# Another PSUM place for two outputs, and an order of steps written anew, in a gated linear attention with an ELU layer

## The chip, the cores and the metric

The kernel runs on one core of one Trainium2 chip. The metric is the device time of one execution in microseconds (us). TensorE (PE, its weight loads PEld), VectorE (DVE), ScalarE (ACT), GpSimd (POOL) and SyncE (SP, which here only issues DMAs) run side by side and meet through semaphores.

## What is computed

The attention has 4 sequences, 8 heads, 768 positions and 48 values a head. In each head a complex state S of 48 x 48 decays by a complex gate a, takes in the outer product of k and v, and is read by q:

```
scale = minimum(mag, 0.999) / (mag + 1e-6)      # mag = |a|
new_re = ar * S_re - ai * S_im                  # ar, ai: gate times scale
new_im = ar * S_im + ai * S_re
S_re, S_im = new_re + kv, new_im                # kv = k[t] outer v[t]
y[t] = q[t] @ S_re
```

Heads side by side give 3072 rows of 384 values, x. Then h = x @ w_in (384 x 2048), g = h where h > 0 and exp(h) - 1 elsewhere, and the result is g @ w_out (2048 x 384). All of it is float32.

## The kernel before

The work is cut into 12 units. A unit is 128 positions of two sequences (NB = 2, numbered n). For each unit the kernel goes from gates to attention, from attention to x, and from x through the two layers.

**Gates.** `squares` (L709, L710) squares the parts of the gate, `joined` (L716) adds them, `logarithms` (L735, L736) and `powers` (L746, L747) form logarithms and exponentials on ScalarE; `lengths` (L772), `ratios` (L759, L760) and `slopes` (L780) are VectorE operations for the first four units, and `ratios` and `joined` are POOL's later. `angles` (L815) is an arctangent on ScalarE and `carried` (L821) adds what came over from the unit before in the sequence. `turns` (`turned`, L832) sums the angles down the positions by a matmul for each n and takes off whole turns on VectorE (L837, L840); its last row goes to a later unit by a POOL DMA (L856). `quartered` (L883) sums the logarithms by matmuls, `quarters_used` (L898) exponentiates them; both are called by `decays` for unit 2 and by `valued` of the unit before for later ones. `waves` (L967 to L971) makes sines and cosines, `scaled` (L981, L982) and `gated` (L993) multiply k and q. `ends` (L951) brings decays at chunk ends into a tile T by way of DRAM.

**Attention.** `transposed` (L1013, copied by ScalarE at L1014) turns q and k over; `state_products` (L1054) and `state_sums` (L1069 on VectorE, L1071 on POOL) carry the states; `scored` (L1126, masked at L1134) makes scores, `valued` the values (L1087) and what the states add (L1096), and ScalarE copies the outcome to x and y (L1157, L1158). `seam` (L1170) moves 16-row pieces of y into their places in x by DMA: three from POOL, three from another queue.

**Layers.** `inner(u, f)` (L1190) is six matmuls of w_in with x, `elu` (L1199 to L1201) makes g. For units 0 and 1 `project(u, n, f0, f1)` (L1211) accumulates g @ w_out for output n over slices f0 to f1 of 16 and, at the last, copies it through two `o` buffers (L1219) to DRAM (L1220). From unit 2 on, folded matmuls (`folded`, `combined`, `product`, L1254 to L1320) take the place of `project`.

**PSUM.** `work` gives tiles from two rings of three: "w" for small results and transposes, and "mlp" for the layers. The tag "y" is one tile of two banks (`[C, 2, 512]`), which scores and values take in turn. A tile that comes round again waits for the last reader of the tile that lay there. Of the four outputs that `project` accumulates, (0, 0), (1, 0) and (0, 1) lie in "mlp", and (1, 1) in "w". SBUF tiles of the gates ("n") come from a ring of six.

**Order.** Each engine works strictly through its instructions in the order in which the program issues them. `first` is a list, written by hand, of calls up to the end of unit 3's gates; `convert` in it takes one step in rounding the weights. After `first`, `plan` sorts steps by due times, and every later unit has the same slots.

Of the kernel before, what the change touches and what calls it, by code (L numbers as in the profile page):

```python
# [10 lines left out]
FP32 = mybir.dt.float32  # L11
# [5 lines left out]
C = 128  # L17
# [488 lines left out]
def kernel(  # L506
# [14 lines left out]
    DM, DF = moe_w_in.shape[0], moe_w_out.shape[0]  # L521
# [3 lines left out]
    NB = 2  # L525
# [11 lines left out]
    ps = ctx.enter_context(tc.tile_pool(name="ps", bufs=1, space=PSUM))  # L537
# [33 lines left out]
    def work(shape, tag="w"):  # L571
        return ps.tile(shape, FP32, tag=tag, bufs=3, name=tag)
# [4 lines left out]
    def where(u):  # L577
        return u % (B // NB) * NB, u // (B // NB) * C
# [114 lines left out]
    def new(tag, bufs=1, shape=None):  # L693
        return sb.tile(shape or [C, NB, H, D], FP32, tag=tag, bufs=bufs, name=tag)
# [510 lines left out]
    def project(u, n, f0, f1):  # L1205
        x = nat[u]
        assert ("out", (f1 - 1) // WF) in done
        if f0 == 0:
            x["o", n] = work([C, DM], "w" if (u, n) == (1, 1) else "mlp")
        for f in range(f0, f1):  # L1210
            nc.tensor.matmul(  # L1211
                x["o", n], lhsT=x["g", f // 8][:, f % 8, ts(n, C)], rhs=w_out[:, f],
                start=(f == 0), stop=(f == NF - 1),
            )
        if f1 == NF:
            b, s = where(u)
            for m in range(2):
                o = new("o", 2, [C, HN])
                nc.scalar.copy(out=o, in_=x["o", n][:, ts(m, HN)])  # L1219
                nc.sync.dma_start(out=out[ds((b + n) * S + s, C), ts(m, HN)], in_=o)  # L1220
# [197 lines left out]
    def gates_of(u, *at):  # L1418
# [37 lines left out]
        (begun, 2), (squares, 2), *2 * [(convert,)], (inner, 1, 8), (inner, 1, 10), (joined, 2),  # L1456
        (convert,), (inner, 1, 12), (fetch, "out", 6), (fetch, "out", 7), *2 * [(convert,)],
        (elu, 1, 8), (convert,), (project, 0, 0, 0, 4), (convert,), (elu, 1, 10),
        *3 * [(convert,)], (elu, 1, 12), (load_qk, 2), *4 * [(convert,)], (inner, 1, 14),
        (elu, 1, 14), (logarithms, 2), (powers, 2), *4 * [(convert,)], (project, 1, 0, 0, 4),  # L1460
        (project, 1, 1, 0, 4), *3 * [(convert,)], (noted, 2), (lengths, 2), (ratios, 2),
        (slopes, 2), (load_a, 3), (angles, 2), (carried, 2), (convert,), (project, 0, 1, 0, 4),
        (convert,), (project, 0, 0, 4, 8), *3 * [(convert,)], (decays, 2), (project, 0, 1, 4, 8),
        *2 * [(convert,)], (turns, 2), (project, 0, 0, 8, 12), (begun, 3), *4 * [(convert,)],
        (project, 1, 0, 4, 8), (waves, 2), (scaled, 2), *2 * [(convert,)], (gated, 2), (ends, 2),
        (load_qk, 3), (squares, 3), *2 * [(convert,)], (project, 1, 1, 4, 8), *4 * [(convert,)],
        (joined, 3), (states, 2, 0), *5 * [(convert,)], (project, 0, 0, 12, 16),
        (transposed, 2, "q", 0), (transposed, 2, "k", 0), (project, 0, 1, 8, 12),
        (transposed, 2, "q", 1), (transposed, 2, "k", 1), (logarithms, 3),
        (project, 1, 1, 8, 12), (scored, 2), (project, 0, 1, 12, 16), (powers, 3), (lengths, 3),  # L1470
        (ratios, 3), (slopes, 3), (angles, 3), (project, 1, 1, 12, 16), (carried, 3),
        (valued, 2), (turns, 3), (project, 1, 0, 8, 12), (seam, 2), (noted, 3), (waves, 3),
        (project, 1, 0, 12, 16), (scaled, 3), (ends, 3), (opened,),
    ]
    def layer_of(u, at_h, at_p):
        for m in range(NF // 2):
# [72 lines left out]
```

## Time and profile before

| what | us |
|---|---|
| median of three runs | 688.48 (686.95 to 689.6) |
| profiled execution | 688.77 |
| its span, first to last instruction | 687.0 |
| PE busy | 661.4 |
| PEld busy | 579.5 |
| DVE busy | 400.5 |
| ACT busy | 396.0 |
| POOL busy | 183.4 |

Busy time is what an engine worked, so several can add up to more than the span. In a timeline a row is a run of like instructions: start, duration, engine, line, output and inputs, how many; in brackets the engine's idle time ahead of it and what ended it. A float32 matmul is two records, so four matmuls of `project` are eight records. Times count from the start of the span. The granted clock is the share of full speed at which TensorE was let run.

### The profile page before, as it was taken

The page shows a single profiled execution, that of the slowest core. Times are in us where ns is not written, and L with a number is a line of the kernel's source. Part 1 is how long each engine was busy: PE and PEld are TensorE (multiplying, and loading weights), DVE is VectorE, ACT ScalarE, POOL GpSimd, SP SyncE. Part 2 cuts the span into 40 slices and gives each one's busy share as a digit, 9 for nine tenths or more (in the row PEclk, how much of TensorE's full clock was granted, in tenths as well). Part 3 has the DMA queues.
Part 4 walks back from the last instruction along what each step waited for, and adds up shares of the span by engine and source line. Part 5 has one row for each costly group of instructions (what it writes and reads, how often), then busy time and mean ns, then how long its engine had stood idle before and what let it go on. Part 6 is the DMA issues. An engine that isn't in the chain of part 4 may idle for free.

```text
span 687.0 us, 15760 instructions
## 1 busy us (share of the span) xinstructions
PE 661.4 (96%) x6656; PEld 579.5 (84%) x6656; DVE 400.5 (58%) x584; ACT 396.0 (58%) x620; POOL 183.4 (27%) x199
## 2 busy tenths in 40 slices
PE   8899899898999999999999999999999999999996
PEld 6777785465889889889889889989989989989996
DVE  5898999815785564564564564654654653642151
ACT  6875455645747657557557557557557557541230
POOL 2000000100233433424424424524524523501000
PEclk9899999899999999999999999999999999999998
DMA  9985655430731741731741731651641631200000
GB/s 167 179 147 91 148 174 160 78 58 25 125 57 53 122 66 54 117 69 53 115 74 52 112 76 51 111 80 51 108 81 50 127 65 49 52 2 7 24 1 29
DMA packets 149899, 55.98 MB, mean 81 GB/s; under 512 B 129172, under 2 KB 142652, under 8 KB 149820
## 3 DMA queue, kind: packets, MB, share of 16 engines
q1 hardware_dynamic: 146336, 53.57, 40.2%
q0 software_dynamic: 3264, 1.18, 1.5%
q8 instruction: 54, 0.88, 0.6%
q14 instruction: 25, 0.20, 0.1%
q10 hardware_dynamic: 220, 0.14, 0.1%
HBM read 48.88 MB, written 4.78 MB: 78 GB/s over the span
## 4 chain that ended last, share of the span: by engine, by line
PE 77%; ACT 1%; issue 1%; DVE 0%; DVEq 0%; ACTq 0%
PE mlp L1190 30%; PE mlp L1296 27%; PE w L1013 5%; PE y L1126 3%; PE w L1054 3%; PE y L1096 3%; PE mlp L1211 3%; PE w L832 2%; PE y L1087 1%; PE w L883 1%; PE w L1211 0%; PE mlp L1054 0%; ACT o L1219 0%; ACT L898 0%; ACT L746 0%
## 5 line engine op out<-in xcount | busy, mean ns | idle before, releaser
L1190 PE MATMUL mlp<-x,w_in 128*128 128x256 f32 x1152 | 262.3, 382 | 2.9 <-DVE g L1201 2.6
L1190 PEld LDWEIGHTS mlp<-x,w_in 128*128 128x128 f32 x1152 | 215.7, 191 | 32.5 <-DVE g L1201 3.0
L1199 ACT ACTIVATE ee<-mlp 128x512 f32<-128x512 f32 x96 | 57.3, 596 | 139.3 <-PE mlp L1190 133.4
L1201 DVE SCALAR_TENSOR_TENSOR g<-ee,mlp 128x512 f32<-128x512 f32 x96 | 65.6, 685 | 119.8 <-ACT ee L1200 107.7
L1296 PE MATMUL mlp<-w_out,g 128*128 128x192 f32 x640 | 110.3, 326 | 0.0
L1296 PEld LDWEIGHTS mlp<-w_out,g 128*128 128x128 f32 x640 | 105.5, 190 | 2.7
L1274 DVE TENSOR_TENSOR g<-g 128x512 f32<-128x512 f32 x80 | 67.4, 842 | 2.7
L1200 ACT ACTIVATE ee<-ee 128x512 f32<-128x512 f32 x96 | 60.5, 630 | 2.8
L1071 POOL TENSOR_TENSOR S<-S,T 128x384 f32<-128x384 f32 x36 | 29.2, 829 | 104.0 <-DVE S L1069 104.0
L1296 PE MATMUL mlp<-w,g 128*128 128x192 f32 x320 | 55.8, 329 | 0.0
L1296 PEld LDWEIGHTS mlp<-w,g 128*128 128x128 f32 x320 | 52.1, 190 | 0.6
L1170 POOL DMA_DIRECT2D x<-y x62 | 30.4, 498 | 70.4 <-ACT y L1111 37.1
L1315 ACT COPY o<-mlp 128x192 f32<-128x192 f32 x10 | 3.2, 318 | 66.0 <-DMA out_dram<-o 32.6
L856 POOL DMA_DIRECT2D carry<-n x10 | 5.0, 504 | 130.5 <-DVE n L840 130.5
L898 ACT ACTIVATE n<-w 64x384 f32<-64x384 f32 (+1 forms) x60 | 28.1, 486 | 18.4 <-PE w L883 17.7
L993 POOL TENSOR_TENSOR kg<-k,cs 128x1536 f32<-128x1536 f32 x8 | 34.9, 4360 | 10.8 <-issue 10.7
L1211 PE MATMUL mlp<-w_out,g 128*128 128x384 f32 x96 | 34.4, 509 | 1.5 <-DVE g L1201 1.5
L716 POOL TENSOR_TENSOR n<-n 128x768 f32<-128x768 f32 x8 | 16.5, 2060 | 69.7 <-ACT n L710 69.7
L1211 PEld LDWEIGHTS mlp<-w_out,g 128*128 128x128 f32 x96 | 18.7, 199 | 15.0 <-issue 2.7
L759 POOL TENSOR_TENSOR n<-ar,n 128x768 f32<-128x768 f32 x8 | 14.9, 1858 | 61.0 <-ACT n L747 61.0
L1296 PE MATMUL mlp<-wt,g 128*128 128x192 f32 x160 | 29.4, 327 | 0.0
L1014 ACT COPY qt<-w 128x512 f32<-128x512 f32 x48 | 25.5, 581 | 5.7 <-PE w L1013 5.7
(173 smaller groups left out, 989.7 us busy)
## 6 DMA issues: line engine op xcount, KB each, us to landing
w<-in_moe_w_out_dram SPq DMA_DIRECT2D x8, 768.0 KB
g<-in_moe_w_in_dram SPq DMA_DIRECT2D x16, 384.0 KB
g<-in_moe_w_out_dram SPq DMA_DIRECT2D x16, 384.0 KB
w<-in_moe_w_in_dram SPq DMA_DIRECT2D x16, 288.0 KB
vn<-in_v_dram SPq DMA_DIRECT2D x24, 192.0 KB
out_dram<-o SPq DMA_DIRECT2D x48, 96.0 KB
ar<-in_a_re_dram SPq DMA_DIRECT2D x22, 192.0 KB
ai<-in_a_im_dram SPq DMA_DIRECT2D x22, 192.0 KB
```

What stands on the lines that cost most here:

```text
L898: nc.scalar.activation(out=flat(x[key][to, n : n + 1]), in_=t[of], func=AF.Exp, scale=sign)
L993: eng.tensor_tensor(out=to[:, :, :, 0:D], in0=each.unsqueeze(2).to_broadcast([C, step * H, 2, D]), in1=x["cs"][:, n * H : (n + step) * H], ...
L1013: nc.tensor.transpose(t[:, h], of, ident)
L1071: eng.tensor_tensor(out=new_s, in0=new_s, in1=wide, op=ALU.mult)
L1170: eng.dma_start(out=x["x"][ds(j * HP + D, G), i], in_=x["y"][ds(j * HP + i * G, G)])
L1190: nc.tensor.matmul(t[:, e], lhsT=w_in[:, i, ts(f + e, C)], rhs=x["x"][:, i], start=(i == 0), stop=(i == NI - 1),)
L1199: nc.scalar.activation(out=e, in_=t, func=AF.Relu, scale=-1.0)
L1200: nc.scalar.activation(out=e, in_=e, func=AF.Exp, scale=-1.0)
L1201: nc.vector.scalar_tensor_tensor(out=x["g", f // 8][:, f % 8 : f % 8 + 2], in0=e, scalar=-1.0, in1=t, op0=ALU.add, op1=ALU.max)
L1211: nc.tensor.matmul(x["o", n], lhsT=x["g", f // 8][:, f % 8, ts(n, C)], rhs=w_out[:, f], start=(f == 0), stop=(f == NF - 1),)
L1274: nc.vector.tensor_tensor(out=S_of(u, k, h), in0=a, in1=b, op=op)
L1296: nc.tensor.matmul(to, lhsT=a[:, m], rhs=b[:, m], start=(first and h == 0 and m == 0), stop=False, skip_group_check=True,)
```

## The change

Outputs of unit 1 no longer come from the two rings. The first call of `project` for unit 1 allocates a "y" tile and gives output 0 its first bank and output 1 its second; outputs of unit 0 stay in "mlp".

```diff
         if f0 == 0:
-            x["o", n] = work([C, DM], "w" if (u, n) == (1, 1) else "mlp")
+            if u == 0:
+                x["o", n] = work([C, DM], "mlp")
+            elif n == 0:
+                t = ps.tile([C, NB, 512], FP32, tag="y", bufs=1, name="y")
+                for m in range(NB):
+                    x["o", m] = t[:, m, 0:DM]
```

The end of `first` is written anew. Unit 1's projections are all done ahead of the scores of unit 2, and unit 0's later slices come after; unit 3's squares stand ahead of unit 2's waves, its logarithms and exponentials right after, its turns ahead of unit 2's values. No step is added or left out. (Units count from 0: the second unit is 1, the fourth is 3.)

```diff
-        (convert,), (project, 0, 0, 4, 8), *3 * [(convert,)], (decays, 2), (project, 0, 1, 4, 8),
-        *2 * [(convert,)], (turns, 2), (project, 0, 0, 8, 12), (begun, 3), *4 * [(convert,)],
-        (project, 1, 0, 4, 8), (waves, 2), (scaled, 2), *2 * [(convert,)], (gated, 2), (ends, 2),
-        (load_qk, 3), (squares, 3), *2 * [(convert,)], (project, 1, 1, 4, 8), *4 * [(convert,)],
-        (joined, 3), (states, 2, 0), *5 * [(convert,)], (project, 0, 0, 12, 16),
-        (transposed, 2, "q", 0), (transposed, 2, "k", 0), (project, 0, 1, 8, 12),
-        (transposed, 2, "q", 1), (transposed, 2, "k", 1), (logarithms, 3),
-        (project, 1, 1, 8, 12), (scored, 2), (project, 0, 1, 12, 16), (powers, 3), (lengths, 3),
-        (ratios, 3), (slopes, 3), (angles, 3), (project, 1, 1, 12, 16), (carried, 3),
-        (valued, 2), (turns, 3), (project, 1, 0, 8, 12), (seam, 2), (noted, 3), (waves, 3),
-        (project, 1, 0, 12, 16), (scaled, 3), (ends, 3), (opened,),
+        (convert,), (project, 0, 0, 4, 8), *3 * [(convert,)], (decays, 2), (project, 1, 0, 4, 8),
+        *2 * [(convert,)], (project, 1, 1, 4, 8), (turns, 2), *2 * [(convert,)],
+        (project, 0, 1, 4, 8), (begun, 3), (squares, 3), *2 * [(convert,)],
+        (project, 1, 0, 8, 12), (waves, 2), (scaled, 2), (joined, 3), (gated, 2), (ends, 2),
+        (load_qk, 3), (logarithms, 3), (powers, 3), (convert,), (project, 1, 1, 8, 12),
+        *4 * [(convert,)], (states, 2, 0), *5 * [(convert,)], (project, 1, 0, 12, 16),
+        (transposed, 2, "q", 0), (project, 1, 1, 12, 16), (transposed, 2, "k", 0), (lengths, 3),
+        (ratios, 3), (slopes, 3), (transposed, 2, "q", 1), (angles, 3), (project, 0, 0, 8, 12),
+        (transposed, 2, "k", 1), (carried, 3), (project, 0, 1, 8, 12), (scored, 2), (turns, 3),
+        (project, 0, 0, 12, 16), (valued, 2), (seam, 2), (noted, 3), (waves, 3),
+        (project, 0, 1, 12, 16), (scaled, 3), (ends, 3), (opened,),
```

The calls of `convert` after the last weights are rounded do nothing. In the order of instructions that the changed program builds, every instruction of the old one is there, and the engines' orders differ only between the sums of logarithms of unit 2 (L883) and the first `inner` of unit 2 (L1190).

## Prediction

> **What bounds the kernel now.** I read the page first, then the chain of waits, then TensorE's timeline between 105 and 176 us, and the timelines of the other engines there.
>
> ```profile
> span 687.0 us, 15760 instructions
> ...
> PE 661.4 (96%) x6656; PEld 579.5 (84%) x6656; DVE 400.5 (58%) x584; ACT 396.0 (58%) x620; POOL 183.4 (27%) x199
> ...
> PE 77%; ACT 1%; issue 1%; DVE 0%; DVEq 0%; ACTq 0%
> ```
>
> TensorE bounds it, so the change can only win where TensorE idles or runs slowly. From 175.87 on the chain is matmuls alone; before that stands the stretch that the change rewrites:
>
> ```profile
> 122.28 2.85 PE L1211 MATMUL mlp<-w_out,g 128*128 128x384 f32 x8
> 127.36 1.65 PE L832 MATMUL w<-n,sum_turns 128*128 128x384 f32 x2 [2.23 <-ACT n L898]
> 129.37 1.65 PE L832 MATMUL w<-n,sum_turns 128*128 128x384 f32 x2 [0.36 <-ACT n L898]
> 130.81 6.91 PE L1211 MATMUL mlp<-w_out,g 128*128 128x384 f32 x16
> ...
> 164.43 1.99 PE L1096 MATMUL y<-qt,S 128*48 128x64 f32 x64
> 168.42 0.88 PE L832 MATMUL w<-n,sum_turns 128*128 128x384 f32 x2 [2.00 <-DVE n L821]
> 169.96 0.91 PE L832 MATMUL w<-n,sum_turns 128*128 128x384 f32 x2 [0.66 <-ACT n L898]
> 170.71 5.32 PE L1211 MATMUL mlp<-w_out,g 128*128 128x384 f32 x16
> 175.87 7.93 PE L1190 MATMUL mlp<-x,w_in 128*128 128x256 f32 x36
> ```
>
> The brackets are idle time. After the first gap, 16 records of L1211 take 6.91 us where the same 16 take 5.32 later. The windows (last three columns: granted clock, DMA share, GB/s) say why:
>
> ```profile
> core 0: us, PE busy (x) PEld busy (x) DVE busy (x) ACT busy (x) POOL busy (x), PEclk, DMA share, GB/s
> 124.00:127.30 3.30, 1.12 (x4) 0.37 (x2) 2.36 (x4) 3.00 (x4) 0.00 (x0) 0.98 1.13 207
> 127.30:134.10 6.80, 6.38 (x10) 3.12 (x11) 6.52 (x10) 4.80 (x8) 1.35 (x2) 0.51 0.08 12
> ```
>
> The first gap costs its idle time and then 6.8 us at half clock. ScalarE's timeline explains the second gap:
>
> ```profile
> 160.34 1.28 ACT L746 ACT_TABLE_LOAD   x1
> ...
> 163.33 1.28 ACT L815 ACT_TABLE_LOAD   x1
> 166.46 0.84 ACT L815 ACTIVATE n<-n 128x768 f32<-128x768 f32 x1 [1.84 <-DVE n L780]
> ```
>
> The fourth unit's exponentials wait at 159.8 behind an output copy; slopes, arctangent and carry follow in series, and the turns come last.
>
> **What the skill says.** "TensorE: Matmul & The Clock Gate", Part 1: a monitor halves the clock after an idle window of about 3.4 us; the trace halves it after only 2.23 us without work, so a window need not be empty. "PSUM — Partial Sum Buffer", PSUM bank collisions: a bank being written must not be read, other banks may; nothing in the trace of before tests it. "ScalarE: Activation LUTs", What ACT_TABLE_LOAD costs: 1.283 us; the trace has 1.28. "DMA: Bandwidth & Descriptors", Anatomy of one DMA: about 2.0 us fixed; the seam's 16 KB took 1.6 to 1.7 from issue to landing.
>
> **TensorE's work without waits.** From 122.28 to 175.87 (53.6 us) the steps, start to start at full clock, are: eleven projections at 2.58 (170.71 to 175.87 holds two), 28.4; two pairs of turns at 1.29 (the later units'), 2.6; two sets of state products at 1.08, 2.2; four transposes at 0.87 (183.64 to 184.51), 3.5; scores 2.0, values 1.1, sums of logarithms 0.8, carried products 1.9. Sum 42.5: hence 11.1 us are stalls and slow clock (idle brackets 6.0, slow clock about 3.4, small drags the rest). No matmul is added. Without any stall, inner(2, 0) would start at 122.28 + 42.5 = 164.8.
>
> **The change, part by part.**
>
> *The y pair.* Before, output (1, 1) holds one of three w slots from 113.6 to 167.5, so the first turn of unit 2 waits until L898 has read a sums tile (127.36). After, its slot is free: it needs L821 (ended 126.10), and TensorE now has two projections ahead of it, 122.28 + 5.16 = 127.4. The second turn needs L898's first tile, ready by then. The gap and the slow clock behind it go. The pair is emptied about 145; its next user, the scores, comes about 153.5. The projection (1, 1, 12, 16) now waits for the copies of output (1, 0): ended 141.45, needed 141.6, zero; should they be late, transposes queue behind it, us for us.
>
> *Squares before waves* (L709, L710, 1.6 us). ScalarE idles 1.75 us before L967, until L840 ends at 132.46; they fit there if a_re and a_im have landed by 129.4, and the DMA share drops to zero at 128.0. Taken: zero; bounds 0 to 0.5. Their join L716 (0.95) fills DVE's gap of 0.88 before L993: 0.1.
>
> *Logarithms and exponentials* (two table loads 2.56, four activations 3.4) take 135.0 to 140.9, inside a ScalarE gap of 7.68 us. The first output copy needs the matmuls of 140.7, so zero. The number of table loads stays.
>
> *Lengths to slopes* (four DVE operations, 3.9) move to 140.7 to 144.6, inside a DVE idle time of 11.48; arctangent to 148.8, carry to end at 150.7. The turns of unit 3 reach TensorE at 155.5: the waits of 2.00, 0.66 and 0.24 go. The second sums tile now waits for a turn's slot to be read (158.5), needed 160.4: zero. POOL and SP keep their sequence (loads, stores, seam); only which output is stored when changes. The ends' rows T (L951, second issue at 134.2, landing after 3.8 to 4.1) are there at 138.3; POOL's L1071, now earlier, needs them at 139.3.
>
> **What is late next.** (1) State products of unit 2 reach TensorE at 136.5, but L993's k gates end about 136.95: 0.55. (2) Copies of output (1, 1) need the two o buffers, thus the stores of (1, 0), issued at 141.3 behind loads that move data until 143.6; before, the pair's data took from 145.3 to 146.5. So about 145.0; the k copy ends 145.85, against a TensorE need at 145.45: 0.45, bounds 0 to 1.5. (3) The seam. Sums end on TensorE at about 161.3; L898 takes 2.9, L1157 and L1158 1.15: x is there at 165.4. Before, the first seam DMA landed 2.0 after that (issue 173.37 after 173.08, plus 1.7), the third by 3.2. TensorE arrives at 161.3 + 1.9 + 2.58 = 165.8, since only one projection covers the seam now, not turns and two. First block 1.6, third another 0.4: 2.0, bounds 1.5 to 2.7 (before, the blocks had landed when matmuls came 2.8 after L1158).
>
> **Sum.** Effective start of inner(2, 0): 164.8 + 0.55 + 0.45 + 2.0 = 167.8, against 175.87: 8.1 us. Afterwards every unit is matmul after matmul in both; the first period has one stall of 0.7 at L1126 that may move (plus or minus 1). Span 687.0 - 8.1 = 678.9; the profiled execution took 688.77, 1.8 outside the span: 680.7. It lay 0.3 above the median of 688.48, so 680.4.
>
> **Rivals.**
>
> *The seam's stall halves the clock.* It is about as long as the gap at 125.1, which did that; the gap at 166.4, 2.00 long, did not. The monitor's windows begin at a phase that may vary. Price: 6.8 us at half clock lose 3.4, as before. 683.8.
>
> *The change doesn't do what it says.* If a wait I count as nothing (loads of a_re, a copy behind a late store, DVE's backlog in unit 2) gives most of it back, the turns still come last: 5 to 8 us back, about 687. Against it: each has its margin above.
>
> *Slower.* ScalarE works in order. If the stores of (1, 0) stay behind the loads, output (1, 1)'s copy blocks the k copies, these the w slots, and TensorE stands. From 145.5 on each us costs one. It decides at 8.1 us of delay, and 0.5% slower needs the stores to land after 157, 15.5 us from issue: about 692. Before, loads of the same size were through 5 us after issue; nothing hints at three times that.
>
> **How the numbers follow.** Forecast 0.74 (678.3 to 682.3: stall bounds plus the moving 1 us); clock rival 0.15; nothing gained 0.08; slower 0.03. The range 678.2 to 684.4 leaves out the last two and the tails. About 0.5%, 3.4 us, is what a measurement of this kernel can tell from no change; faster by that means under 685.0. Both first cases are, and a part of the third: 0.91; same 0.06, slower 0.03.
>
> **What would show it.** The first turn of unit 2 right behind matmuls near 127.4, with the clock at 1.0 in 127 to 134; L815 of unit 3 near 149; turns of unit 3 without a wait before the values; inner(2, 0) at about 167.5, idle some 1.6 to 2 us before it, waiting for DMA. Wrong: a long wait of L1014 or the output copies about 141 to 148, half clock after 166, or unit periods over 52 us afterwards.

## The result, and the profile after

The changed kernel takes 681.66 us, the median of 4 runs (681.41 to 682.32), against 687.72 (686.72 to 689.6, 4 runs) for the kernel before, launched beside it: a ratio of 0.991, 95% interval 0.9885 to 0.9935. That is faster by 0.9%, and the interval leaves out no change. Its profiled execution took 681.87, with a span of 680.1 (before: 687.0).

The page of the changed kernel; the second line is each engine's busy time, share of the span and count of instructions, the third the chain of waits by engine:

```profile
span 680.1 us, 15754 instructions
...
PE 657.5 (97%) x6656; PEld 578.1 (85%) x6656; DVE 400.9 (59%) x584; ACT 395.9 (58%) x620; POOL 184.2 (27%) x199
...
PE 82%; DVE 9%; ACT 4%; issue 3%; DMA 1%; ACTq 0%; POOL 0%; DVEq 0%; POOLq 0%
```

The same 6656 matmuls are there, and PE's busy time is 3.9 us less (661.4 to 657.5): a matmul at half clock counts as busy for longer (the 16 records of L1211 took 6.91 us before, where the same 16 take 5.32 elsewhere), so part of the gain does not look like idle time at all. The 6.9 us of the span divide as follows. I call the stretch from the sums of logarithms of unit 2 (L883) to the first transposes of unit 3 (L1013) the stage. It took 183.64 - 121.47 = 62.17 us before and 177.30 - 121.89 = 55.41 after, which is 6.76 less. What lies ahead of it is 0.42 longer, what follows 0.56 shorter (687.0 - 183.64 = 503.36 against 680.1 - 177.30 = 502.80).

TensorE's timeline of the changed kernel in the stage (start, duration, engine, line, operation, tiles, shape, count, and in brackets the idle time ahead of it and who ended it):

```profile
121.89 0.88 PE L883 MATMUL w<-n,sum_logs 64*64 64x384 f32 x8
122.70 5.43 PE L1216 MATMUL y<-w_out,g 128*128 128x384 f32 x16
127.96 1.45 PE L832 MATMUL w<-n,sum_turns 128*128 128x384 f32 x4
...
131.83 5.32 PE L1216 MATMUL y<-w_out,g 128*128 128x384 f32 x16
137.34 1.15 PE L1054 MATMUL w<-vn,kg 64*64 64x48 f32 x64 [0.18 <-DVE kg L993]
...
145.45 0.60 PE L1013 MATMUL w<-ident,qg 128*128 128x128 f32 x4
147.26 0.66 PE L1013 MATMUL w<-ident,qg 128*128 128x128 f32 x4 [1.22 <-ACT kt L1014]
...
156.98 1.56 PE L832 MATMUL w<-n,sum_turns 128*128 128x384 f32 x4
...
164.71 2.85 PE L1216 MATMUL mlp<-w_out,g 128*128 128x384 f32 x8
169.13 8.34 PE L1190 MATMUL mlp<-x,w_in 128*128 128x256 f32 x36 [1.57 <-DMA x<-y]
177.30 1.04 PE L1013 MATMUL w<-ident,qg 128*128 128x128 f32 x8
```

Both pairs of turns (L832) now follow matmuls with no idle time before them; before, they waited 2.23 and 0.36, then 2.00 and 0.66. Two new waits have come: 1.22 before the second half of a set of transposes, and 1.57 at the seam (from start to start, the projection ahead of L1190 takes 1.84 us longer than the usual 2.58). The windows of the changed kernel show that the slow clock after the first turns is gone (PEclk is the first of the last three columns):

```profile
core 0: us, PE busy (x) PEld busy (x) DVE busy (x) ACT busy (x) POOL busy (x), PEclk, DMA share, GB/s
124.00:128.00 4.00, 4.00 (x14) 2.31 (x13) 3.06 (x4) 3.21 (x5) 0.00 (x0) 1.00 1.12 206
128.00:132.00 4.00, 4.00 (x14) 2.41 (x13) 3.75 (x7) 3.72 (x7) 0.00 (x0) 1.00 0.09 14
132.00:136.00 4.00, 4.00 (x13) 2.31 (x13) 3.95 (x6) 3.87 (x5) 2.38 (x3) 1.00 0.07 2
```

ScalarE's timeline of the changed kernel holds the reason for the first new wait:

```profile
140.53 0.83 ACT L747 ACTIVATE n<-n 128x768 f32<-128x768 f32 x1
141.30 0.54 ACT L1224 COPY o<-y 128x192 f32<-128x192 f32 x2
141.73 1.08 ACT L1014 COPY qt<-w 128x512 f32<-128x512 f32 x2
146.16 0.56 ACT L1224 COPY o<-y 128x192 f32<-128x192 f32 x2 [3.34 <-PE w L1013]
146.62 1.08 ACT L1014 COPY kt<-w 128x512 f32<-128x512 f32 x2
...
149.99 0.85 ACT L815 ACTIVATE n<-n 128x768 f32<-128x768 f32 x1
```

The two copies at 146.16 are those of output (1, 1). ScalarE stood idle for 3.34 us ahead of them. The releaser named, a transpose on PE, is not what they read: output (1, 1)'s own matmuls were over at 144.74. What they waited for, as I read it, is the stores that empty the `o` buffers. SP's timeline of the changed kernel shows when those stores went out:

```profile
140.02 2.82 SPq L596 DMA_DIRECT2D k<-in_k_dram  x2
142.94 19.42 SPq L1225 DMA_DIRECT2D out_dram<-o  x6
```

The first store stands behind the two loads of k, whose issue took 2.82 us where it took 1.56 before. The copies of k (L1014) queue behind the output's on ScalarE, and TensorE behind them. Experiment 1 tests this reading, and in experiment 4 the profile itself names the stores.

### The profile page after: what moved, and what is told of

Same layout as the page of the kernel before. It is cut to its first block, busy times and chain, and to the rows that moved or that the text cites. A ratio compares the mean times of both kernels' runs of the same rounds, so it can differ in the third digit from the quotient of the medians.

```text
span 680.1 us, 15754 instructions
## 1 busy us (share of the span) xinstructions
PE 657.5 (97%) x6656; PEld 578.1 (85%) x6656; DVE 400.9 (59%) x584; ACT 395.9 (58%) x620; POOL 184.2 (27%) x199
## 4 chain that ended last, share of the span: by engine, by line
PE 82%; DVE 9%; ACT 4%; issue 3%; DMA 1%; ACTq 0%; POOL 0%; DVEq 0%; POOLq 0%
PE mlp L1190 33%; PE mlp L1301 27%; PE w L1013 6%; PE y L1096 3%; PE y L1126 3%; PE w L1054 3%; PE y L1087 2%; PE w L832 2%; DVE wf L43 1%; DVE w_out L653 1%; DVE wp L50 1%; DVE g L1201 1%; PE mlp L1404 1%; PE y L1216 1%; PE w L883 1%
## 5 line engine op out<-in xcount | busy, mean ns | idle before, releaser
L1190 PE MATMUL mlp<-x,w_in 128*128 128x256 f32 x1152 | 262.6, 382 | 4.6 <-DVE g L1201 2.7
L1190 PEld LDWEIGHTS mlp<-x,w_in 128*128 128x128 f32 x1152 | 215.5, 191 | 34.8 <-DVE g L1201 3.1
L1301 PEld LDWEIGHTS mlp<-w_out,g 128*128 128x128 f32 x640 | 105.5, 190 | 2.7
L993 POOL TENSOR_TENSOR kg<-k,cs 128x1536 f32<-128x1536 f32 x8 | 34.8, 4351 | 12.6 <-issue 12.5
L759 POOL TENSOR_TENSOR n<-ar,n 128x768 f32<-128x768 f32 x8 | 14.9, 1861 | 61.0 <-ACT n L747 61.0
L1013 PE MATMUL w<-ident,qg 128*128 128x128 f32 x192 | 26.3, 283 | 1.9 <-ACT kt L1014 1.2
L993 DVE TENSOR_TENSOR qg<-q,cs 128x1536 f32<-128x1536 f32 (+1 forms) x12 | 19.5, 1622 | 14.8 <-ACT cs L971 14.8
L821 DVE SCALAR_TENSOR_TENSOR n<-carry,n 1x768 f32<-1x768 f32 x10 | 9.5, 947 | 31.5 <-ACT n L815 31.5
```

The source lines that it names most:

```text
L993: eng.tensor_tensor(out=to[:, :, :, 0:D], in0=each.unsqueeze(2).to_broadcast([C, step * H, 2, D]), in1=x["cs"][:, n * H : (n + step) * H], ...
L1013: nc.tensor.transpose(t[:, h], of, ident)
L1190: nc.tensor.matmul(t[:, e], lhsT=w_in[:, i, ts(f + e, C)], rhs=x["x"][:, i], start=(i == 0), stop=(i == NI - 1),)
L1301: nc.tensor.matmul(to, lhsT=a[:, m], rhs=b[:, m], start=(first and h == 0 and m == 0), stop=False, skip_group_check=True,)
```

## The experiments

Theory: the gain is the end of the turns' waits, one half by unit 2's turns standing behind ready work (idle time and slow clock), the other by unit 3's gates being done early; what is missing is paid at the store wait and at the seam. Rivals: the y pair is what brings the gain; the place of the turns in TensorE's queue, not the early gates, brings the second half; the missing part is scatter and not those two waits.

The time before the stage varies between executions of kernels that are the same up to there: the stage began between 119.68 and 124.54 in the traces below, at least in part because stretches at half clock in the first 90 us fall differently (one of 6.8 us in the execution that began at 119.68, four adding to 20.5 us in one that began at 124.38). A timed median of a few runs holds that scatter. Medians are compared through their ratios to the kernel before, since experiments 1 to 4, 5 to 8, and 9 and 10 ran on three chips, each beside its own runs of the kernel before (687.91, 689.21 and 688.34 us). I give beside each median two lengths from the trace, both from the start of L883: to the first `inner` of unit 2 (54.40 before, 47.24 after) and the stage (62.17 and 55.41).

### 1. The copies of output (1, 1) in a tile of their own

```diff
+            spare_o = new("ee", 2, [C, 2, GT]) if (u, n) == (1, 1) else None
             for m in range(2):
-                o = new("o", 2, [C, HN])
+                o = spare_o[:, m, 0:HN] if spare_o is not None else new("o", 2, [C, HN])
```

> The changed kernel, with one edit: the copies of output (1, 1) go into a free ee tile, not into the two o buffers that the stores of output (1, 0) still read. Theory: in the changed kernel ScalarE stood 3.34 us before those copies, the k copies behind them came late and TensorE lost 1.22 us (1.34 with its restart) at the second half of q's transposes; all of it is on the path, so this run is 1.3 us faster than the changed kernel's 681.7, at 680.4, with TensorE's wait near 146 gone. Rival: what ends last there is ScalarE's own chain up to x and the seam, so the stall moves to the seam (about 1.6 us becomes 2.9) and the time stays at 681.7.

Measured: 680.85 (679.11 to 685.47, 6 runs), ratio 0.9903 [0.9873, 0.9934]. To the first `inner`: 45.84, 1.40 less than after. Stage: 55.70, 0.3 more. TensorE's timeline of this kernel:

```profile
145.99 1.07 PE L1013 MATMUL w<-ident,qg 128*128 128x128 f32 x8
...
168.27 10.03 PE L1190 MATMUL mlp<-x,w_in 128*128 128x256 f32 x36 [1.57 <-DMA x<-y]
```

All eight transposes run through: the wait was for the `o` buffers, and it cost 1.4. The seam's wait stays at 1.57, so the rival of the expectation, that the stall would move there, is out. But the 36 matmuls at 168.27 took 10.03 us where after has 8.34. The windows of this kernel say why:

```profile
165.00:169.30 4.30, 2.63 (x9) 1.28 (x8) 1.83 (x2) 4.21 (x8) 2.79 (x5) 1.00 0.10 24
169.30:172.70 3.40, 3.40 (x9) 2.69 (x8) 2.59 (x2) 1.20 (x3) 0.56 (x1) 0.50 0.47 72
172.70:176.00 3.30, 3.30 (x17) 2.87 (x16) 1.11 (x2) 2.76 (x4) 0.00 (x0) 1.00 1.12 205
```

The seam's stall, as long as in after (1.57), was followed here by 3.4 us at half clock (9 matmuls in 3.40 us, then 17 in 3.30). This is the prediction's first rival, at half its price.

### 2. The seam covered by two projections

```diff
-        (transposed, 2, "k", 1), (carried, 3), (project, 0, 1, 8, 12), (scored, 2), (turns, 3),
-        (project, 0, 0, 12, 16), (valued, 2), (seam, 2), (noted, 3), (waves, 3),
+        (transposed, 2, "k", 1), (carried, 3), (scored, 2), (turns, 3), (project, 0, 1, 8, 12),
+        (valued, 2), (seam, 2), (project, 0, 0, 12, 16), (noted, 3), (waves, 3),
```

> The changed kernel, with one edit in the list: projection (0, 1, 8, 12) moves behind the turns of unit 3, and (0, 0, 12, 16) behind the values and the seam, so that two projections (5.16 us) instead of one (2.58) stand between the carried products and the first matmul that reads x. Theory: the seam's wait is only lack of cover, 1.57 us before the first matmul, 0.25 more than worked out at its restart and 0.4 in the first ones: about 2.2 us go, 679.5. Rival: the moved projections uncover another wait instead (values waiting for masks, or the copies of the last k transpose), 1 us or more comes back, 681 to 682.

Measured: 681.32 (678.89 to 684.05, 6 runs), ratio 0.9900 [0.9873, 0.9927]. To `inner` 45.63, stage 53.40, 2.0 less than after. TensorE's timeline of this kernel:

```profile
149.59 0.66 PE L1013 MATMUL w<-ident,qg 128*128 128x128 f32 x4 [1.07 <-ACT kt L1014]
...
170.01 7.93 PE L1190 MATMUL mlp<-x,w_in 128*128 128x256 f32 x36
```

The store wait stays (1.07), the seam's is gone, and the 36 matmuls take 7.93 as before the change. The median does not show it. This profiled execution (682.77) began its stage at 124.38, late by the slow clock of its start; whether that explains the other runs too is not known. A little of the rival came true: the second set of state products takes 1.4 from start to start instead of 1.1.

### 3. Both

> Both edits: the free tile for the copies of (1, 1), and two projections over the seam. Theory: the two stalls are one after the other on TensorE and add up, 1.3 + 2.2: 678.2. Rival: they are two ends of one chain on ScalarE, so both together give no more than the better of the two: 679.5 or above.

Measured: 679.17 (677.67 to 680.96, 4 runs), ratio 0.9865 [0.9838, 0.9892]. To `inner` 44.72, stage 52.82. Neither stall is left but for 0.20 at the seam:

```profile
167.43 8.26 PE L1190 MATMUL mlp<-x,w_in 128*128 128x256 f32 x36 [0.20 <-DMA x<-y]
```

The two edits together are worth 55.41 - 52.82 = 2.6 us of stage. That is more than the better one gives alone (2.0), so they are not two ends of one chain, but less than the sum of 1.4 and 2.0 that the theory had. The difference is mostly at the seam again, where TensorE now arrives sooner: 0.20 is idle, and the 36 matmuls take 8.26 instead of 7.93.

### 4. The new order alone, outputs in their old places

The list of steps is that of the changed kernel; output (1, 0) keeps its place in mlp and (1, 1) its w slot.

```diff
-            if u == 0:
-                x["o", n] = work([C, DM], "mlp")
-            elif n == 0:
-                t = ps.tile([C, NB, 512], FP32, tag="y", bufs=1, name="y")
-                for m in range(NB):
-                    x["o", m] = t[:, m, 0:DM]
+            x["o", n] = work([C, DM], "w" if (u, n) == (1, 1) else "mlp")
```

> The new order of steps, with the outputs of unit 1 in their old places (three in mlp, one in w). Theory: the w slot that output (1, 1) holds makes the second turn of unit 2 wait for the reads of the second sums tile (ready near 129.8, TensorE there at 128.6), 1.2 us, and costs something at the transposes, 0.5 to 1.5: 683.5 to 684.5, with the clock at full in 127 to 134, since the gap is shorter than the 2.23 us of the old kernel. Rival: without the pair the gap and the half clock come back whole, 685.5 or more; other rival: the pair is not needed at all, 681.7.

Measured: 680.53 (679.88 to 681.68, 5 runs), ratio 0.9895 [0.9872, 0.9918]. To `inner` 47.02, stage 55.20. My theory fell, and its second rival held: the kernel is as fast as the changed one. TensorE's timeline of it:

```profile
126.88 0.81 PE L832 MATMUL w<-n,sum_turns 128*128 128x384 f32 x2
128.71 0.91 PE L832 MATMUL w<-n,sum_turns 128*128 128x384 f32 x2 [1.03 <-ACT n L898]
...
145.47 1.15 PE L1013 MATMUL w<-ident,qg 128*128 128x128 f32 x8
...
167.83 8.34 PE L1190 MATMUL mlp<-x,w_in 128*128 128x256 f32 x36 [1.57 <-DMA x<-y]
```

Without the pair the second turn does wait, 1.03. But the k copies then make no one wait: TensorE comes to them 1 us later, and the store was issued 0.26 us sooner after L883 than in after (141.60 - 120.81 = 20.79 against 21.05, with k's issue at 1.64 us). ScalarE's timeline of this kernel has the same wait for the stores, here under its own name:

```profile
144.88 0.54 ACT L1219 COPY o<-w 128x192 f32<-128x192 f32 x2 [2.10 <-DMA out_dram<-o]
```

So the y pair removes one wait and the store wait takes its place.

### 5. Of the kernel before, only unit 2's turns behind the next projection

```diff
-        *2 * [(convert,)], (turns, 2), (project, 0, 0, 8, 12), (begun, 3), *4 * [(convert,)],
+        *2 * [(convert,)], (project, 0, 0, 8, 12), (turns, 2), (begun, 3), *4 * [(convert,)],
```

> The kernel before, with one edit: the turns of unit 2 stand behind the next projection, nothing else. It tests whether the first gap (2.23 us and 0.36) and the slow clock behind it are what the change won most from. The stretch from the sums of unit 2 (L883) to the first transposes of unit 3 (L1013) took 62.2 us before and 55.4 after. Theory: the gap shrinks to 1.3 us (second turn waiting for the second sums tile), the clock stays full, but then the state products wait 1.7 us for k's gates, whose time doesn't move; 3.3 us of the 6.8 are won, the stretch takes 58.9 and the time is 684.6 against 687.9. Rival: the chain of unit 3's gates sets the end of the stretch whatever TensorE does before, so the stretch and the time stay at 62.2 and 687.9.

Measured: 686.47 (683.88 to 689.8, 22 runs) against 689.21 (687.35 to 694.73, 27 runs), ratio 0.9959 [0.9945, 0.9973]. To `inner` 51.40, stage 59.17: both 3.0 less than before. TensorE's timeline of this kernel:

```profile
127.66 0.81 PE L832 MATMUL w<-n,sum_turns 128*128 128x384 f32 x2
129.51 0.91 PE L832 MATMUL w<-n,sum_turns 128*128 128x384 f32 x2 [1.04 <-ACT n L898]
...
137.03 1.15 PE L1054 MATMUL w<-vn,kg 64*64 64x48 f32 x64 [1.45 <-DVE kg L993]
```

The first gap (2.23 and 0.36) became 1.04, and no half clock followed; 1.45 came back at the k gates, to which TensorE now comes sooner. This exchange of two list entries alone brings 3.0, where the change brings 6.76. That the half clock belongs to the gap, and is no accident of one trace, is borne out by the granted clock on record for every execution: its mean is 0.9841 over the 27 of the kernel before and 0.9881 over the 22 of this one. The difference, 0.0040, is near the 0.0049 that 6.8 us at half clock make in 687 us.

### 6. The changed kernel with unit 3's gates late

```diff
-        (project, 0, 1, 4, 8), (begun, 3), (squares, 3), *2 * [(convert,)],
-        (project, 1, 0, 8, 12), (waves, 2), (scaled, 2), (joined, 3), (gated, 2), (ends, 2),
-        (load_qk, 3), (logarithms, 3), (powers, 3), (convert,), (project, 1, 1, 8, 12),
-        *4 * [(convert,)], (states, 2, 0), *5 * [(convert,)], (project, 1, 0, 12, 16),
...
+        (transposed, 2, "k", 1), (logarithms, 3), (project, 0, 1, 8, 12), (scored, 2),
+        (powers, 3), (lengths, 3), (ratios, 3), (slopes, 3), (angles, 3),
+        (project, 0, 0, 12, 16), (carried, 3), (valued, 2), (turns, 3), (seam, 2), (noted, 3), (waves, 3),
```

> The changed kernel with its pair and its order of projections, but unit 3's squares, logarithms, exponentials, lengths to carry and turns where the old list had them in relation to unit 2's steps. Theory: the turns of unit 3 wait for a carry that ends near 166 (about 2.6 us of idle), and the sums are exponentiated behind the arctangent, so x comes later too: first matmul of x near 172.2 instead of 169.1, 3.1 us back, 684.8, stretch 58.5. Rival: the projections and the pair made the whole gain, and the gates' early place none: 681.7, stretch 55.4.

Measured: 684.54 (681.9 to 686.95, 6 runs), ratio 0.9931 [0.9907, 0.9955]. To `inner` 48.98, stage 58.84. TensorE's timeline of this kernel:

```profile
164.60 0.91 PE L832 MATMUL w<-n,sum_turns 128*128 128x384 f32 x2 [1.32 <-DVE n L821]
166.23 0.91 PE L832 MATMUL w<-n,sum_turns 128*128 128x384 f32 x2 [0.72 <-ACT n L898]
...
171.39 10.02 PE L1190 MATMUL mlp<-x,w_in 128*128 128x256 f32 x36 [1.67 <-DMA x<-y]
```

The waits of unit 3's turns are back, 1.32 and 0.72 together 2.04, as the theory has it. To `inner` it costs 1.74 net: the 2.04 and slower restarts behind these waits, less 0.70 by which the store wait fell (to 0.52). The other 1.7 of the stage is the half clock behind the seam again (10.02 against 8.34), so the 58.84 agrees with the expected 58.5 only by that accident. Experiments 5 and 6 account for 3.0 and 1.74 of the 7.16 us that the change gains to `inner`. The other 2.4 belong to the rest of the new order and no run takes them apart; the timelines show one part, that five projections and not four stand ahead of unit 2's state products, so that the wait for k's gates is 0.18 where experiment 5 has 1.45.

### 7. The order alone, with the copies of output (1, 1) in a tile of their own

The edit of experiment 1 on the kernel of experiment 4.

> The new order, with unit 1's outputs in their old places, and the copies of (1, 1) in a free ee tile. With the order alone the stretch took 55.2 us, with 1.03 us idle at the second turn but no wait at q's second transposes; with the pair 55.4, none at the turns and 1.22 at the transposes. Theory: the two cancelled each other by chance, since the order alone started its stores 1.3 us earlier, so that without the wait for the stores the pair is worth its 1.1 us: this run stays at 55.2 and 680.5, while pair and free tile together reached the first matmul of x in 45.8 us after L883 (47.0 here). Rival: the pair is worth nothing, and this run reaches it in 45.8 too.

Measured: 682.27 (681.25 to 684.18, 5 runs) against 689.21, ratio 0.9897 [0.9878, 0.9916]. To `inner` 46.89, stage 55.06. TensorE's timeline of this kernel:

```profile
132.47 0.91 PE L832 MATMUL w<-n,sum_turns 128*128 128x384 f32 x2 [1.05 <-ACT n L898]
...
149.14 1.07 PE L1013 MATMUL w<-ident,qg 128*128 128x128 f32 x8
```

As expected, the other buffers bring next to nothing without the pair (46.89 against 47.02). (The 1.3 us by which the expectation has the order alone start its stores sooner are 0.26 when counted from L883; the rest was the earlier start of the stage.) With experiment 1 (45.84) this makes a square: the pair is worth 1.05 once the store wait is gone, which is the 1.05 of the turn's wait here, and nothing while it is there (47.24 against 47.02).

### 8. The changed kernel with unit 3's turns behind the values

```diff
-        (transposed, 2, "k", 1), (carried, 3), (project, 0, 1, 8, 12), (scored, 2), (turns, 3),
-        (project, 0, 0, 12, 16), (valued, 2), (seam, 2), (noted, 3), (waves, 3),
+        (transposed, 2, "k", 1), (carried, 3), (project, 0, 1, 8, 12), (scored, 2),
+        (project, 0, 0, 12, 16), (valued, 2), (turns, 3), (seam, 2), (noted, 3), (waves, 3),
```

> The changed kernel with one edit: the turns of unit 3 go back behind the values, as the old list had them. Theory: early turns save nothing by then (the carry ends at 151.8, long before), and taken from between carried products and x they are missing as cover: 1.4 us of the seam's wait go, first matmul of x 45.8 us after L883 instead of 47.2, stretch 54.0, time 680.3. Rival: turns behind the values make waves and q's gates of unit 3 late, and what the seam gives back the first transposes of unit 3 lose: stretch 55.4, 681.7.

Measured: 683.35 (680.63 to 685.69, 6 runs) against 689.21, ratio 0.9907 [0.9884, 0.993]. To `inner` 47.54, stage 57.15. TensorE's timeline of this kernel:

```profile
148.64 0.66 PE L1013 MATMUL w<-ident,qg 128*128 128x128 f32 x4 [1.16 <-ACT kt L1014]
...
164.79 1.56 PE L832 MATMUL w<-n,sum_turns 128*128 128x384 f32 x4
...
170.88 9.77 PE L1190 MATMUL mlp<-x,w_in 128*128 128x256 f32 x36 [1.95 <-DMA x<-y]
```

The ratio is that of the changed kernel, which is the time that the rival of the expectation gave, but not where it put the loss: it is at the seam and not at unit 3's first transposes. I had expected the late turns to cover the seam as a projection does. They do fill TensorE for 1.4 us between the values and the seam, and do not wait; but the seam came later by as much. GpSimd's timeline of this kernel shows how:

```profile
168.44 0.54 POOL L856 DMA_DIRECT2D carry<-n  x1 [7.84 <-DVE n L840]
169.19 1.45 POOL L1170 DMA_DIRECT2D x<-y  x3 [0.20 <-PE mlp L1216]
```

The carry of the late turns goes out on the same queue ahead of the seam's pieces and waits for the last L840. y was ready (L1158 ended at 167.18), and in the changed kernel the pieces went out 0.3 after that (167.38 after 167.08); here 2.0 after. What the cover gave, the queue took. Another 1.4 in the stage is half clock once more (9.77 against 8.34). The run also settles a rival from the head of this section: with the gates early, turns in their old place wait for nothing (47.54 to `inner`, against 48.98 with the gates late in experiment 6), so it is the early gates, and not the place of the turns, that end the second wait.

### 9 and 10. The changed kernel and the version of experiment 3 again, on one chip

> The changed kernel itself, once more, beside the version with both further edits. The theory: the changed kernel stands 6 us below the kernel before (ratio 0.991), with 55.4 us from the first sum of logarithms of unit 3's predecessor to the first transposes of unit 3 if the clock stays full there, and 1.2 to 1.7 us more where the stall of 1.6 us at the seam halves the clock. The rival: it is no slower than the version with both edits, whose lower time on another chip was chance.

> The version with the copies of output (1, 1) in buffers of their own and two projections moved behind the sums and the seam, again. If the two stalls (1.3 us before the k copies, 1.6 to 2.0 at the seam) are what the changed kernel still pays, it stays 2 to 3 us below the changed kernel on the same chip (stage 52.8 against 55.4). The rival: the medians of the two agree within 0.7 us.

Measured, against 688.34 (686.68 to 690.02, 11 runs): the changed kernel 682.05 (678.49 to 683.68, 6 runs), ratio 0.9898 [0.9871, 0.9924]; with both edits 678.75 (677.84 to 679.32, 4 runs), ratio 0.9862 [0.9839, 0.9886]. The changed kernel's timeline on TensorE in this second profiled execution:

```profile
146.94 0.66 PE L1013 MATMUL w<-ident,qg 128*128 128x128 f32 x4 [1.35 <-ACT kt L1014]
...
168.82 10.02 PE L1190 MATMUL mlp<-x,w_in 128*128 128x256 f32 x36 [1.58 <-DMA x<-y]
```

and that of the version with both edits:

```profile
143.24 1.07 PE L1013 MATMUL w<-ident,qg 128*128 128x128 f32 x8
...
164.44 8.31 PE L1190 MATMUL mlp<-x,w_in 128*128 128x256 f32 x36 [0.20 <-DMA x<-y]
```

The lengths to `inner` repeat (47.35 and 44.76, first 47.24 and 44.72). The medians stand 3.3 us apart. The two intervals overlap a little (0.9871 to 0.9886), but experiment 3 gave the same distance from the kernel before (0.9865), and the traces show where it lies: of 4.3 us between the two stages, 2.6 are the stalls up to `inner`, and 1.7 half clock. It is the fastest kernel of this study, 1.4% below the kernel before. The changed kernel's stage is 57.21 this time, by the half clock: the same program with the same stall (1.57 and 1.58) had full clock in one execution and half in another.

## Why the prediction was right, step by step

*TensorE's work without waits.* From the start of L883 the unstalled stage is 0.81 + 42.5 + 7.77 = 51.08 (7.77 is 175.87 to 183.64 before). The best version took 52.82 and 52.91, so 1.7 to 1.8 us are left for its small waits, and nothing contradicts the sum of 42.5.

*The y pair.* Both turns of unit 2 came as told (127.96 for 127.4, nothing idle, clock 1.0). What failed is the cause: the prediction booked the whole first gap and its slow clock under the pair. Experiments 4 and 7 show that the new order alone removes the first part and the slow clock, and the pair the last 1.05, which the store wait then takes back. The number does not suffer, as the change has both.

*Squares, logarithms and exponentials at zero.* Right: on ScalarE the last exponential ended at 141.36, and the first output copy stood at 141.30 right behind it, with no idle time on TensorE. *Lengths to carry*: L815 at 149.99 (told: near 149), and unit 3's turns without a wait. Putting those steps back costs 2.04 of idle time and 1.74 net (experiment 6).

*What is late next.* The three places were right, the sizes were not:

| Term, us | Predicted | After | How it is read |
|---|---|---|---|
| k gates (L993) | 0.55 | about 0.35 | L1054 at 137.34, the projections' steps end at 131.83 + 5.16 |
| Store wait | 0.45 (0 to 1.5) | 1.34 | 145.45 + 0.47 to 147.26; experiment 1: 1.40 |
| Seam, with the third block | 2.0 (1.5 to 2.7) | 2.25 | 164.71 + 2.58 to 169.13 is 1.84; 8.34 - 7.93 is 0.41 |
| Small drags | 0 | about 0.4 | the rest |

Stage told: 62.17 - 8.1 = 54.1; measured 55.41. The 1.3 between them are 0.9 from the store wait, 0.25 from the seam and 0.4 from drags, less 0.2 from the k gates. The term mis-sized is the store wait. The step in it was "issued at 141.3 behind loads that move data until 143.6": the stores were issued at 142.94 (of which 0.42 is the later start of the stage), since the loads of k took 2.82 to issue and not the 1.56 of before. The landing, once issued, was quicker than told (146.16 is 3.2 later, against 3.7). The span came out at 680.1 for 678.9: those 1.3, 0.4 ahead of the stage, and 0.5 gained back in later units, inside the plus or minus 1 that the prediction left for later units. The forecast's upper end of 682.3 was drawn tighter than its own bounds: put one on another, 0.5 for the squares, 1.05 for the store wait, 0.7 for the seam and 1 for later units would reach 683.6.

*The rivals.* That the slow clock follows the seam's stall got a chance of 0.15 and a price of 3.4. In the seven profiled executions with a seam wait of 1.57 or more (the changed kernel twice, experiments 1, 4, 6, 7 and 8) it followed in four, and it cost 1.4 to 1.7 (9.77 to 10.03 for the 36 matmuls, against 8.34), as it lasts 3.4 us (experiment 1) and not 6.8. So it is common and half as dear as I had it. What it adds to the medians of the changed kernel, 681.66 and 682.05 where 680.4 was told, is not shown: the profiled execution with full clock at the seam took 681.87, so the mis-sized terms alone reach as far, and no run holds the clock fixed. Luck has a part in it: what got a chance of 0.15 came in four executions of seven, and the time stayed near the forecast because it costs half of the price that was told. "The Trainium skill", "TensorE: Matmul & The Clock Gate", Part 1, speaks of an idle window of about 3.4 us before the halving; here idle times of 1.57 to 1.95 were followed by it in four executions of seven, and the runs leave open what decides. The other two rivals did not occur.

*Left open.* Why the k loads take longer to issue: 2.47 to 3.21 us in all eight traces with the y pair, 1.56 to 1.95 in all four without. SP's stream is the same and the loads come at the same distance from L883 (18.1 us in the changed kernel and in experiments 4 and 7), so the slower issue goes with the pair; by what way, no experiment shows. There is no run of the pair with the old order: there the scores of unit 2 would use the pair's bank before output (1, 0) is complete.

## What to carry to other kernels

When a stall is removed from the bounding engine, list the next waits in order of time, and price each with what queues ahead of it on every queue (here a store behind two loads, a copy behind the store, other copies behind that copy); two waits in series replace each other, so an edit worth 1 us alone can show nothing until the next one is gone. Keep independent work behind the last producer before a DMA, as cover for its landing: moving two projections took 2.0 us off this stage, while the turns, whose own DMA is queued ahead of the seam's, gave nothing. And judge effects of 1 to 3 us by a stage's length in the trace beside the timed median, since slow clock elsewhere shifts the median by as much.

## What I had not expected of the hardware

VectorE and GpSimd slowed each other. VectorE's timeline of the changed kernel has, in unit 3's moved lengths and ratios,

```profile
140.84 0.95 DVE L772 SCALAR_TENSOR_TENSOR n<-n 128x768 f32<-128x768 f32 x1
141.71 1.58 DVE L759 TENSOR_TENSOR n<-ar,n 128x768 f32<-128x768 f32 x1
```

and GpSimd's timeline of it, at the same time,

```profile
139.50 0.83 POOL L1071 TENSOR_TENSOR S<-S,T 128x384 f32<-128x384 f32 x1 [3.92 <-DVE S L1069]
141.01 1.47 POOL L1071 TENSOR_TENSOR S<-S,T 128x384 f32<-128x384 f32 x1 [0.67 <-DVE S L1069]
```

L759 took 1.58 instead of the 0.95 that it had alone before the change, and the second state sum 1.47 instead of 0.83. It is so in all nine traces in which they meet (1.58 or 1.59, and 1.47 or 1.48), and in none of the kernel before and experiments 5 and 6, where they don't. "The Trainium skill", "SBUF — State Buffer", Who interferes with whom, says that the two engines share a port pair under an exclusive lock, and the trace agrees: the operations look as if they took turns. The sum began while L772 ran, and ended 0.69 after L772's end at 141.79; L759 began while the sum ran, and ended 0.81 after the sum's end at 142.48. In experiment 6 L772 meets a sum that began first: the sum keeps its 0.83, and L772 takes 1.27. It cost nothing here, as the table load for the arctangent that waits for L780 began only at 148.70. The second surprise is the clock: a stall of the same length in the same program is followed by 3.4 us at half speed in one execution and by none in another.
